# Four shared two-bank PSUM buffers for attention, casts and division sums that heed GpSimd's port, and a new order of the work

## The chip, the cores and the metric

The kernel runs on one core of one Trainium2 chip. The metric is device time in microseconds (us) of one execution. Three executions of the kernel before took 958.71, 961.17 and 962.71 us; the median, 961.17 us, is the time before.

## The reference, cut to what matters

Attention in which a query sees only the keys of its own hash bucket, and behind it a gated feed-forward layer:

```python
q_bits = (einsum('bhsd,dk->bhsk', q, proj) > 0)          # 6 bits; k_bits likewise
mask   = q_bucket[:, :, :, None] == k_bucket[:, :, None, :]
scores = where(mask, q @ k.T / sqrt(64), -1e9)
attn   = exp(scores - max);  attn = attn / (sum(attn) + 1e-9)
x      = attn @ v                                       # 4 x 8 heads, 768 tokens, 64 wide
out    = (sigmoid(x @ w_gate) * (x @ w_val)) @ w_out    # 3072 tokens, 512 -> 1536 -> 512
```

All is fp32. The kernel splits an operand into a high and a low part in fp32r where one pass would not be exact enough.

## The kernel before, in words

**Stages.** Sixteen pairs of heads go through attention one after the other (`pair`, line 808), each in two groups of three query tiles of 128 rows (`attend`, line 1066). Beside it the weights of the feed-forward layer are read as 64-bit numbers, converted, split and stored again (`converted`, `split`, `combined`, lines 363 to 493). Behind attention comes the feed-forward layer (`moe_pair`, line 726), whose seven products per block are Strassen-like sums.

**Tasks of attention.** TensorE does, per group: six *scores* tasks (letter `s`: `scores`, line 1072, eight matmuls in row tiles of 64, into a two-bank PSUM tile `sc`), six *turns* (`t`: `turned`, line 1126, 36 passes of transposes in row tiles, into a two-bank tile `tp`) and six *values* (`v`: `values`, line 1148, in column tiles of 64, all six accumulating into one tile `pv`). Per pair there are two turns of the inputs (`q`: `turn`, line 917) and a hash (`h`: `hash_`, line 956). `f` is an idle matmul (`busy`, line 331); there are 24. VectorE takes the maximum of `sc` (line 1095), ScalarE the exponent (line 1103), VectorE or ScalarE copy `tp` to `ef` (line 1143) and `pv` to `xs` (line 1160), and GpSimd multiplies `xs` with the reciprocal of the sums (line 1163). The sums get their reciprocals in `inverse` (line 1108): add 1e-9, reciprocal, transpose, on VectorE. The high part of q and k is a cast of 128x768 from SBUF to SBUF on ScalarE or VectorE (`high`, line 943); the low part is a subtraction on GpSimd or VectorE (`low`, line 947).

**PSUM.** Attention has three two-bank buffers (`banks`, line 325; in the plan `two=range(3)`) for `sc`, `tp`, the turned inputs and the hash, and two one-bank buffers (pool `ps`, tag `one`), of which the idle matmuls hold one until the last of them; `pv` and the first pair's hash of q take these. Eight banks in all. The first products of the feed-forward layer (`opening`, line 622) use the two one-bank buffers.

**Order.** The order of every engine's instructions is worked out before the kernel is built, by `Plan.order` (line 99). TensorE's order in attention is written out as the string `ORDER`, a letter per task; behind it come the feed-forward tasks in the order in which they were added. On the other engines, of the tasks that are ready the one with the lowest key goes first; `SHIFTS` adds a number to the key of single tasks. A task can only start in the plan when what it takes is free: a PSUM buffer, an SBUF slot, or the token `port`, which GpSimd's operations and some of VectorE's take. On the chip nothing enforces the token: there the engines run their lists in order and wait only for data and for buffers.

```python
    def inverse():
        some = gz["su"][:, : 2 * GT]
        nc.vector.tensor_scalar_add(some, some, EPS)
        nc.vector.reciprocal(some, some)
```

Of the kernel before, what the change touches and what calls it, by code (L numbers as in the profile page):

```python
# [44 lines left out]
    "ffffffffqqqqhhqqhssssshqqfffffffsssssffffhtsstfftttvvvtqqffftsshssssvvtttvvttsssvvvttstssqqvvvvtthtt"  # L45
    "sssvvvtttvvtstsssssvsstvvvsttvvtttvqqssshvtsssvvvtttvvtttssssvvvvvttststtvvvqqtvvttsssssvshvtttvvsts"
    "tssssvqqvtttvvttsssvssvvtttvvttssssvhstvvvttssvvtttvvqqtsshsssstvvvtttvvttsvvvttsssssvvtttvvvqsqsvtt"
    "tvstssshvvvvtttstssssstvvvtttvvvqqstvssshvststvtttvvttssssssvvtqqvvvttttsssssvvvvvthsttvvtttvttsssss"
    "svvvqttvvvttttqssssvvshvvtttsssvssvvvttssttvvqvqttsssssvvvhttttvvttssssvtsssvvvtttvtqqvvvttssssvsstv"
    "htttvvttsssssvvsttvvtqqvvtthtsssssvvvtttvvttssssvvtssstvvvvvtttqqtstsssssvvvtvvvtthttssssvttvvsttvvt"  # L50
    "tsssvvvvtsstvssttvvttsssvttsssvvvvtttvvttvttvvvvtttvvvv"
)
SHIFTS = {
    158: -2.2, 334: -14.55, 652: 23.1, 1364: 2.85, 1375: 12.45, 1713: 14.4, 1743: 15.05, 1759: 14.3, 1800: 16.1, 1830: -10.7,
    1880: -24.2, 1953: 10.2, 1982: 4.8, 2032: 24.05, 2063: 18.85, 2064: 6.9, 2254: 5.25,
# [25 lines left out]
class Plan:  # L81
# [17 lines left out]
    def order(self):  # L99
# [25 lines left out]
        while events:  # L125
            now = events[0][0]
            while events and events[0][0] <= now:
                _, _, kind, what = heapq.heappop(events)
                if kind == "ready":
                    for m, (e, _, _) in enumerate(what.options):  # L130
                        key, number = what.key
                        heapq.heappush(ready[e], ((key + m * SECOND, number), what))
                elif kind == "give" and isinstance(what, tuple):
                    self.rooms[what[0]].append(what[1])
                elif kind == "give":
                    self.stock[what] += 1
            again = True
            while again:
                again = False
                for e in SEEN:  # L140
                    if free[e] > now:
                        continue
                    held = []
                    if e == "pe":
                        t = turns[-1] if turns and any(x is turns[-1] for _, x in ready[e]) and free_for(turns[-1]) else None
                        if t is not None:
                            turns.pop()
                            ready[e] = [kx for kx in ready[e] if kx[1] is not t]
                        held = []
                    while ready[e] and e != "pe":  # L150
                        key, t = heapq.heappop(ready[e])
                        if t.started:
                            continue
                        first = t.options[0][0]
                        behind = sum(not x.started for _, x in ready[first]) if first != e else BEHIND
                        if behind >= BEHIND and free_for(t):
                            break
                        held.append((key, t))
                    else:
                        t = t if e == "pe" else None  # L160
                    for h in held:
                        heapq.heappush(ready[e], h)
                    if t is None:
                        continue
                    again = t.started = True
                    for r in t.take:
                        if r in self.rooms:
                            t.room = self.rooms[r].pop(0)
                        else:
                            self.stock[r] -= 1  # L170
                    ns, emit = next((x[1], x[2]) for x in t.options if x[0] == e)
                    if e == "pe":
                        ns += (LEAVE + BEGIN[t.kind]) * (tiles != t.tiles)
                        last, tiles = t.kind, t.tiles
                    free[e] = now + ns
                    landed, more = 0, ()
                    if t.dmas:
                        n_, moved, *more = t.dmas
                        if e == "sp":
                            free[e] = max(now, self.landings[0]) + ns  # L180
                        self.moving = max(self.moving, free[e] - ns + BEFORE) + moved
                        landed = max(self.moving, free[e] + BEFORE // 2) + BEHIND_IT - free[e]
                        if e == "sp":
                            self.landings = (self.landings + [free[e] + landed] * n_)[n_:]
                    at(free[e], "free", e)
                    seen = free[e] + (landed + sum(more) if landed else SEEN[e])
                    for r in t.give:
# [12 lines left out]
                    out.append((now, emit, e, ns, t.room))  # L200
# [5 lines left out]
def lsh_attention_glu_kernel(ctx, tc, q, k, v, proj, w_gate, w_val, w_out, out):  # L206
# [41 lines left out]
    ps = ctx.enter_context(tc.tile_pool(name="ps", bufs=2, space=PSUM))  # L248
# [71 lines left out]
    for m in range(3):  # L320
        nc.gpsimd.memset(sums[m], 0.0)
# [3 lines left out]
    def banks(name):  # L325
        return ps2.tile([P, 2, 512], F32, name=name, tag=f"two{plan.room}")


    idle = ps.tile([P, 512], F32, name="idle", tag="one")

    def busy():
# [4 lines left out]
        one=1, two=range(3), z=6, kr=2, qr=2, vr=2, h=2, e=12, st=3, su=3, sv=2, rb=2, xs=2,  # L336
# [277 lines left out]
    def group(key, u, n, js, x, sig_, final, prev):  # L614
# [111 lines left out]
    def moe_pair(key, u, prev):  # L726
# [8 lines left out]
        def part_(t, js):  # L735
            pool, tag_ = (ps, "one") if t % TC < ONES else (later["ps"], "z")
# [71 lines left out]
    def pair(i):  # L808
# [171 lines left out]
        def first_pair(needs):  # L980
# [11 lines left out]
            for n, p_ in (("k", 0), ("q", 0), ("k", 1), ("q", 1)):  # L992
# [11 lines left out]
                hash__[n, p_] = add(n_ + 0.1, "pe", 4 * MM * (1 + (n == "k" and p_ == 0)), lambda n=n, p_=p_: hash_first(n, p_), after=[x_, hw["task"]], take=["one"] if n == "q" else ["two"] * (1 - p_), kind="first", stream="h")  # L1004
                b_ = add(n_ + 0.2, "dve", 620, lambda n=n, p_=p_: bits_first(n, p_), after=[hash__[n, p_]], give=["one"] if n == "q" else [("two", hash__["k", 0])] * p_)
                h_ = add(n_ + 0.1, [("act", 430, lambda n=n, p_=p_: high_half(n, p_, nc.scalar.copy)), ("dve", 300, lambda n=n, p_=p_: high_half(n, p_, nc.vector.tensor_copy))], after=[x_])
# [3 lines left out]
                if n == "q":  # L1010
# [4 lines left out]
                    sh = add(n_ + 0.4, [("act", 430, lambda p_=p_: high_half("qs", p_, nc.scalar.copy)), ("dve", 300, lambda p_=p_: high_half("qs", p_, nc.vector.tensor_copy))], after=[s_])  # L1015
# [50 lines left out]
    def attend(i, g, z, needs, v_here):  # L1066
# [21 lines left out]
        def maximum(t, h):  # L1088
# [3 lines left out]
            if h == 0:  # L1092
# [102 lines left out]
        prev = None  # L1195
        for c in range(NC):
            prev = add(
                n if c == 0 else OPEN, "pe", FF, lambda c=c: values(c), after=[prev, v_here, chunks[c]], take=["one"] if c == 0 else [],
                kind="values", give=["ef"] + (["vr"] if c == NC - 1 and g == NG - 1 else []),
            )  # L1200
        a = add(n - 6, either(summed), after=[prev], take=["xs"], give=["one"])
# [4 lines left out]
    for m in range(FILL):  # L1206
        add(IDLE, "pe", MO + (m < WARM) * MO + (m == 0) * 1300, busy, give=["one"] * (m == FILL - 1), stream="f")
# [3 lines left out]
    every = [a for s_ in stored.values() for a in s_]  # L1211

# [37 lines left out]
    for u in range(PAIRS):  # L1250
# [3 lines left out]
        prev = moe_pair(2e4, u, prev)  # L1254

# [33 lines left out]
```

## Time and profile before

| | |
|---|---|
| median of three executions | 961.17 us |
| the profiled execution's own time | 959.54 us |
| span from its first to its last instruction | 957.7 us |
| TensorE busy | 941.2 us (98%) |
| VectorE busy | 765.5 us (80%) |
| ScalarE busy | 497.6 us (52%) |
| GpSimd busy | 249.6 us (26%) |
| granted TensorE clock | 1.00 throughout |

A matmul's end in the profile is modelled, so TensorE at 98% can still wait; the distance from the start of one task to the start of the next is the surer reading. Engines are named PE (TensorE), PEld (its weight loads), DVE (VectorE), ACT (ScalarE), POOL (GpSimd) and SP (SyncE, which issues the DMAs). A tile's name stands for all its buffers.

### The profile page before, as it was taken

The numbers are of one execution on the slowest core, as the hardware profiler recorded it, in microseconds if no ns is written. First come the engines' busy times: TensorE is split into PE (matmuls) and PEld (weight loads), VectorE is DVE, ScalarE is ACT, GpSimd is POOL, SyncE is SP. The second block draws the span as 40 slices with busy tenths as digits, with TensorE's granted clock in tenths as the row PEclk, the third lists the DMA queues.
The fourth block names the chain that finished last, engine by engine and source line by source line (L and its number), as shares of the span: only waits on it lengthen the run. The fifth ranks groups of instructions, "written<-read, shape, count | busy, mean of one in ns | idle before, by whom it ended". The sixth has DMA issues, their size and how long they took to land.

```text
span 957.7 us, 19418 instructions
## 1 busy us (share of the span) xinstructions
PE 941.2 (98%) x7536; PEld 700.4 (73%) x7536; DVE 765.5 (80%) x1362; ACT 497.6 (52%) x868; POOL 249.6 (26%) x227
## 2 busy tenths in 40 slices
PE   8999999998999999999999999999999999999998
PEld 4666666565666666678888888888888888888886
DVE  8989999999999999976867679745766785666566
ACT  6889888898898888854323133231222323221120
POOL 5365465565565555111331100000000000000000
PEclk9999999999999999999999999999999999999999
DMA  6677867777578656678776545844455464554412
GB/s 181 176 226 235 249 210 226 231 216 242 183 240 252 180 190 210 245 294 289 267 251 233 173 148 205 314 147 145 133 194 176 142 232 132 198 166 152 140 60 88
DMA packets 112132, 190.87 MB, mean 199 GB/s; under 512 B 38664, under 2 KB 70824, under 8 KB 112040
## 3 DMA queue, kind: packets, MB, share of 16 engines
q1 hardware_dynamic: 111880, 189.63, 61.3%
q8 instruction: 59, 0.97, 0.4%
q14 instruction: 33, 0.27, 0.1%
q10 hardware_dynamic: 160, 0.00, 0.0%
HBM read 135.27 MB, written 41.42 MB: 185 GB/s over the span
## 4 chain that ended last, share of the span: by engine, by line
PE 88%; DVE 7%; DMA 2%; ACT 1%; issue 1%; SPq 0%; POOL 0%; DVEq 0%; ACTq 0%; POOLq 0%
PE yo L744 19%; PE pv L1153 12%; PE sc L1083 9%; PE tp L1136 7%; PE sc L1077 4%; PE z3g L637 3%; PE z1g L637 3%; PE z2v L637 3%; PE z7g L637 3%; PE z1v L637 3%; PE z4g L637 3%; PE z5g L637 3%; PE z2g L637 3%; PE z6g L637 3%; PE z4v L637 2%; PE z7v L637 2%
## 5 line engine op out<-in xcount | busy, mean ns | idle before, releaser
L1103 ACT ACTIVATE e<-e,st 128x768 f32<-128x768 f32 x192 | 178.3, 930 | 24.4 <-DVE e L1095 24.0
L1095 DVE TENSOR_SCALAR_CACHE_REDUCE e<-sc 128x768 f32<-128x768 f32 x192 | 174.3, 951 | 6.6 <-PE sc L1083 5.2
L1153 PE MATMUL pv<-ef,vr 128*64 128x384 f32 x768 | 143.1, 498 | 0.0
L775 DVE TENSOR_TENSOR ol<-yo,ol 128x512 f32<-128x512 f32 x120 | 82.0, 689 | 54.9 <-PE yo L744 54.7
L1136 PEld LDWEIGHTS tp<-ident,e 64*128 64x128 f32 x2304 | 81.6, 139 | 46.3 <-DVE e L1095 9.8
L1143 ACT COPY ef<-tp 128x768 f32<-128x768 f32 x113 | 87.8, 798 | 21.7 <-PE tp L1136 21.0
L1136 PE MATMUL tp<-ident,e 64*128 64x64 f32 x2304 | 93.6, 227 | 1.4 <-DVE ef L1143 1.0
L1083 PE MATMUL sc<-kh,qsl 64*128 64x384 f32 x192 | 89.8, 468 | 0.0
L1083 PE MATMUL sc<-kh,ql 64*128 64x384 f32 x192 | 89.8, 468 | 0.0
L1153 PEld LDWEIGHTS pv<-ef,vr 128*64 128x64 f32 x768 | 47.3, 136 | 52.4 <-issue 46.2
L1143 DVE COPY ef<-tp 128x768 f32<-128x768 f32 x79 | 74.4, 952 | 7.4 <-PE tp L1136 6.7
L1077 PE MATMUL sc<-kb,qb 64*128 64x384 bf16 x384 | 65.0, 329 | 7.2 <-DVE ef L1143 4.1
L1083 PE MATMUL sc<-kh,qh 64*128 64x384 f32 x192 | 64.3, 335 | 0.0
L1083 PE MATMUL sc<-kh,qsh 64*128 64x384 f32 x192 | 64.2, 334 | 0.0
L1083 PE MATMUL sc<-kl,qh 64*128 64x384 f32 x192 | 64.0, 334 | 0.0
L1083 PE MATMUL sc<-kl,qsh 64*128 64x384 f32 x192 | 64.0, 333 | 0.0
L701 ACT COPY snm1v<-z1v 128x512 f32<-128x512 f32 x18 | 10.6, 589 | 100.9 <-PE z1v L637 100.9
L666 DVE TENSOR_TENSOR gf(0, 0)v<-z2v,snm1v 128x512 f32<-128x512 f32 x18 | 12.5, 692 | 54.9 <-PE z2v L637 54.9
L1077 PEld LDWEIGHTS <-qb 64*128 64x128 bf16 x384 | 23.2, 94 | 40.4 <-issue 30.2
L1163 POOL TENSOR_TENSOR xs<-xs,rb 128x384 f32<-128x384 f32 x32 | 35.3, 1102 | 42.4 <-DVE xs L1160 25.0
L744 PE MATMUL yo<-wo,hh00v 128*128 128x512 f32 x144 | 44.3, 389 | 0.0
L744 PE MATMUL yo<-wo,hh10v 128*128 128x512 f32 x144 | 44.3, 389 | 0.0
(268 smaller groups left out, 2462.2 us busy)
## 6 DMA issues: line engine op xcount, KB each, us to landing
wg<-kg SPq DMA_DIRECT2D x54, 512.0 KB
wv<-kv SPq DMA_DIRECT2D x54, 512.0 KB
wo<-ko SPq DMA_DIRECT2D x36, 512.0 KB
kg<-pkg SPq DMA_DIRECT2D x18, 512.0 KB
kv<-pkv SPq DMA_DIRECT2D x18, 512.0 KB
vr<-in_v_dram SPq DMA_DIRECT2D x16, 384.0 KB
rawg<-in_moe_w_gate_dram SPq DMA_DIRECT2D x12, 512.0 KB
rb<-rd SPq DMA_DIRECT2D x64, 96.0 KB
```

The lines of the kernel that those rows point to most:

```text
L637: nc.tensor.matmul(bank[m], a[:, wc], x[xx, block][:, c, :], start=(c == 0 and i == 0), stop=(c == 1 and i == 2),)
L666: nc.vector.tensor_add(tile_(name, tag) if tag else z[name], bank[m], z[y])
L744: nc.tensor.matmul(accs[t], a[:, ts_], w, start=(jj == 0 and q == 0), stop=(jj == 1 and q == 2),)
L775: FIRST, "dve", 610, lambda t=t: nc.vector.tensor_add(obs[t], accs[t], obs[t]), after=[prev, ended_[t]],
L1077: nc.tensor.matmul(sc[:, j, :GN], z["qb"][rows, beyond if j else c], z["kb"][rows, h], start=True, stop=False, tile_position=(j * D, 0),)
L1083: nc.tensor.matmul(sc[:, j, :GN], q_[rows, c], z["k" + x][rows, h * GN : (h + 1) * GN], start=False, stop=(m == 2), tile_position=(j * D, 0),)
L1095: nc.vector.tensor_scalar(sp(e), gz["sc", t, h][:, :, :GN], MASKED, None, op0=ALU.min, op1=ALU.min, accum_out=gz["st", t][:, h : h + 1],)
L1103: nc.scalar.activation(e, e, AF.Exp, bias=st[:, h : h + 1], scale=-1.0, accum_out=gz["su"][:, h * GT + t : h * GT + t + 1],)
L1136: nc.tensor.transpose(tp[:, r, at_ : at_ + D], gz["e", t, h][rows, c * P : (c + 1) * P], ident[rows, rows], tile_position=(r * D, 0),)
L1143: copy(gz["ef", c].rearrange("p (n r d) -> p r n d", r=2, d=D), gz["tp", c][:, :, :GN].rearrange("p r (n d) -> p r n d", d=D),)
L1153: nc.tensor.matmul(gz["pv"][rows, :GN], z["v"][:, h, 2 * (c % GT) + c // GT], gz["ef", c][:, h * GN : (h + 1) * GN], start=(c == 0), stop= ...
L1163: nc.gpsimd.tensor_mul(gz["xs"], gz["xs"], gz["rb"])
```

## The change

Five things are done.

1. The two one-bank buffers become a fourth two-bank buffer (number 3, pool `psd`). It serves all of attention like the other three. `pv` and the first pair's hash of q now take one of the four, of which they use the first bank. The idle matmuls hold number 3 until the last of them. A new task of SyncE, `ones_switch`, takes number 3 after the last scores and turns it into the two one-bank buffers that the feed-forward layer uses.
2. On VectorE the casts of the high parts (`high`, and `high_half` of the first pair) take the token `port` in the plan; on ScalarE they don't.
3. In `inverse` the tensor-scalar addition of 1e-9 is replaced by a reduction over pairs: columns 0 to 5 of `su` hold the sums, columns 6 to 11 hold 1e-9 (the memset at the start writes it), and a `tensor_reduce` adds the two into a tile `inv`. The reciprocal and the transpose work on `inv`. A further memset writes `inv` once.
4. `ORDER` is another string with as many letters of each kind.
5. `SHIFTS` has 2199 entries in place of 17, for tasks of all stages.

```diff
 ORDER = (
-    "ffffffffqqqqhhqqhssssshqqfffffffsssssffffhtsstfftttvvvtqqffftsshssssvvtttvvttsssvvvttstssqqvvvvtthtt"
-    "sssvvvtttvvtstsssssvsstvvvsttvvtttvqqssshvtsssvvvtttvvtttssssvvvvvttststtvvvqqtvvttsssssvshvtttvvsts"
...
-    "tsssvvvvtsstvssttvvttsssvttsssvvvvtttvvttvttvvvvtttvvvv"
+    "fffffqqqqhqhhqshsssffsqqffssssffffftthtssstffffvttvvvvvqtqffffffsttsstsstvvvvtsssvvhstsssttvtstvvvtts"
+    "qvvqtstthssstvvvvtsssvvttststsvtvvssqvvvvsttsqtsssthvttvvvvvststtsstvvsstvvtqqvssssvhtttstvvvttssssv"
...
+    "vvvtttsvtvsttvvttsssvssssvssvsttvtttvvvvvtttvttvttvvvvv"
 )
 SHIFTS = {
-    158: -2.2, 334: -14.55, 652: 23.1, 1364: 2.85, 1375: 12.45, 1713: 14.4, 1743: 15.05, 1759: 14.3, 1800: 16.1, 1830: -10.7,
...
+    24: -34.3, 25: 3.05, 26: 17.6, 27: 67.8, 29: 26.45, 31: 4.55, 33: 17.1, 34: 2.35, 37: 32.55, 39: 14.15, 40: 32.5,
...
 }
-        def free_for(t):
-            return all((len(self.rooms[r]) if r in self.rooms else self.stock[r]) >= t.take.count(r) for r in t.take)
+        def also(t, e):
+            return next((x[3] for x in t.options if x[0] == e and len(x) > 3), [])
+        def free_for(t, e):
+            return all(
+                r[1] in self.rooms[r[0]] if isinstance(r, tuple) else (len(self.rooms[r]) if r in self.rooms else self.stock[r]) >= t.take.count(r)
+                for r in t.take
+            ) and all(self.stock[r] >= 1 for r in also(t, e))
...
-    ps = ctx.enter_context(tc.tile_pool(name="ps", bufs=2, space=PSUM))
+    psd = ExitStack()
+    ps = psd.enter_context(tc.tile_pool(name="psd", bufs=1, space=PSUM, side="right"))
...
-        nc.gpsimd.memset(sums[m], 0.0)
+        nc.gpsimd.memset(sums[m], EPS)
+    inv = const.tile([P, 32], F32, name="inv")
+    nc.gpsimd.memset(inv, 0.0)
...
-        return ps2.tile([P, 2, 512], F32, name=name, tag=f"two{plan.room}")
+        return (ps if plan.room == 3 else ps2).tile([P, 2, 512], F32, name=name, tag=f"two{plan.room}")
-    idle = ps.tile([P, 512], F32, name="idle", tag="one")
+    idle = ps.tile([P, 2, 512], F32, name="idle", tag="two3")[:, 0]
...
-        one=1, two=range(3), z=6, kr=2, qr=2, vr=2, h=2, e=12, st=3, su=3, sv=2, rb=2, xs=2,
+        one=0, two=range(3), z=6, kr=2, qr=2, vr=2, h=2, e=12, st=3, su=3, sv=2, rb=2, xs=2,
...
-            pool, tag_ = (ps, "one") if opening else (later["ps"], "z")
+            pool, tag_ = (later["one"], "one") if opening else (later["ps"], "z")
...
-                z["hs", n, m] = ps.tile([P, 512], F32, name=f"h{n}{m}{u}", tag="one")
+                z["hs", n, m] = banks(f"h{n}{m}{u}")[:, 0]
...
-            b_ = add(n_, [("act", 735, lambda n=n: high(n, nc.scalar.copy)), ("dve", 480, lambda n=n: high(n, nc.vector.tensor_copy))],
+            b_ = add(n_, [("act", 735, lambda n=n: high(n, nc.scalar.copy)), ("dve", 480, lambda n=n: high(n, nc.vector.tensor_copy), ["port"])],
...
-            some = gz["su"][:, : 2 * GT]
-            nc.vector.tensor_scalar_add(some, some, EPS)
-            nc.vector.reciprocal(some, some)
+            with_eps = gz["su"][:, : 4 * GT].rearrange("p (m n) -> p n m", m=2)
+            nc.vector.tensor_reduce(inv[:, : 2 * GT], with_eps, axis=AX.X, op=ALU.add)
+            nc.vector.reciprocal(inv[:, : 2 * GT], inv[:, : 2 * GT])
             gz["sv"] = at.tile([P, 32], F32, name=f"sv{u}", tag="sv", bufs=stock["sv"])
-            nc.vector.transpose(gz["sv"], gz["su"])
+            nc.vector.transpose(gz["sv"], inv)
...
-                gz["pv"] = ps.tile([P, 512], F32, name=f"pv{u}", tag="one")
+                gz["pv"] = banks(f"pv{u}")[:, 0]
...
-        a = add(n - 6, either(summed), after=[prev], take=["xs"], give=["one"])
+        a = add(n - 6, either(summed), after=[prev], take=["xs"], give=[("two", first_)])
...
+    a.room = 3
+    a.give = [("two", a)]
...
+    def ones_switch():
+        psd.close()
+        later["one"] = ctx.enter_context(tc.tile_pool(name="ps", bufs=2, space=PSUM, side="right", reuse_waits="tile"))
...
+    add(0, "sp", 0, ones_switch, after=score_tasks["last"], take=[("two", 3)], give=["one", "one"])
```

## Rows read from the trace of the kernel before

**Rows 1.** Busy time by stretch: start:end, length, each engine's busy us (instructions), clock, DMA.

```profile
25.00:412.70 387.70, 379.55 (x4965) 242.02 (x4961) 363.45 (x726) 332.28 (x603) 209.10 (x179) 1.00 0.72 222
412.70:957.70 545.00, 539.75 (x2378) 445.63 (x2376) 380.90 (x570) 148.89 (x234) 27.43 (x25) 1.00 0.54 184
```

**Rows 2.** Timeline of TensorE: first idle matmuls, first feed-forward product (start, us).

```profile
1.31 3.59 PE L332 MATMUL idle<-zero 128*128 128x512 bf16 x8 [1.31 <-POOL zero L260]
...
412.71 0.50 PE L637 MATMUL z1g<-a11h,wg 128*128 128x512 f32 x1
```

**Rows 3.** Chain of waits up to 420 us: runs of values and turns (start, us).

```profile
70.35 0.80 PE pv L1153 x4
...
96.64 3.38 PE pv L1153 x20
100.02 0.89 PE tp L1136 x24
...
127.03 1.28 PE tp L1136 x36
```

**Rows 4.** Timeline of TensorE at 156 us: two scores, a hash, the next scores.

```profile
155.97 0.34 PE L1077 MATMUL sc<-kb,qb 64*128 64x384 bf16 x2
156.66 0.34 PE L1077 MATMUL sc<-kb,qb 64*128 64x384 bf16 x2
157.47 0.51 PE L960 MATMUL hs<-qx,hw 128*32 128x384 f32 x1
...
158.25 0.34 PE L1077 MATMUL sc<-kb,qb 64*128 64x384 bf16 x2
```

**Rows 5.** Groups by line, VectorE to 413 us: xcount | busy us, mean ns | idle before.

```profile
L1110 DVE TENSOR_SCALAR su<-su 128x6 f32<-128x6 f32 x32 | 9.7, 302 | 1.7 <-ACT e L1103 1.7
L945 DVE CAST qh<-qx 128x768 fp32r<-128x768 f32 x9 | 9.6, 1069 | 0.2
L945 DVE CAST kh<-kx 128x768 fp32r<-128x768 f32 x7 | 6.6, 946 | 0.1
```

**Rows 6.** Single lines: shortest/median/longest ns, first and last start in us.

```profile
L945 DVE CAST qh<-qx x9: 549/792/2206, 17.2 to 357.4; 128x768 fp32r<-128x768 f32 x9
L1110 DVE TENSOR_SCALAR su<-su x32: 159/168/1769, 22.0 to 404.1; 128x6 f32<-128x6 f32 x32
L1111 DVE RECIPROCAL su<-su x32: 191/192/194, 22.2 to 404.3; 128x6 f32<-128x6 f32 x32
```

**Rows 7.** Timelines at 229 us: GpSimd's subtraction, VectorE's addition, TensorE's next scores.

```profile
228.82 2.12 POOL L948 TENSOR_TENSOR ql<-qx,qh 128x768 fp32r<-128x768 f32 x1
...
229.20 1.77 DVE L1110 TENSOR_SCALAR su<-su 128x6 f32<-128x6 f32 x1
...
232.33 0.34 PE L1077 MATMUL sc<-kb,qb 64*128 64x384 bf16 x2 [2.23 <-DVE ef L1143]
```

**Rows 8.** TensorE's waits from 25 us to 412.7 us: us in total, times, longest.

```profile
PE sc L1077 <- DVE ef L1143: 4.1, 3, 2.2
```

**Rows 9.** Single lines that take the token: shortest/median/longest ns, first and last start.

```profile
L388 DVE TENSOR_SCALAR exg<-rawg x12: 416/425/818, 29.2 to 448.3; 128x512 int32<-128x512 int32 x12
...
L395 DVE TENSOR_SCALAR mfg<-rawg x12: 409/420/440, 29.6 to 448.6; 128x512 int32<-128x512 int32 x12
```

**Rows 10.** A reduction of the setup, as in rows 9.

```profile
L292 DVE TENSOR_REDUCE picked<-ident x4: 167/168/179, 2.5 to 3.2; 128x1 f32<-128x24 f32 x4
```

**Rows 11.** Timelines of the opening: VectorE's cast at 17 us, TensorE at 20 us.

```profile
17.20 2.21 DVE L945 CAST qh<-qx 128x768 fp32r<-128x768 f32 x1
...
20.33 0.34 PE L1077 MATMUL sc<-kb,qb 64*128 64x384 bf16 x2 [0.59 <-DVE e L1095]
```

**Rows 12.** Timelines between attention and feed-forward: VectorE twice, TensorE.

```profile
399.42 1.23 DVE L537 TENSOR_TENSOR a11l<-ra,a11h 128x1024 fp32r<-128x1024 f32 x1 [0.28 <-ACT a11h L533]
...
416.45 1.22 DVE L537 TENSOR_TENSOR s4l<-ra,s4h 128x1024 fp32r<-128x1024 f32 x1
...
419.28 0.47 PE L637 MATMUL z3g<-s4h,wg 128*128 128x512 f32 x1 [0.83 <-issue]
```

More of the change, by code (lines that the diff above doesn't have):

```diff
@@ L129, in order @@
                 if kind == "ready":
-                    for m, (e, _, _) in enumerate(what.options):
+                    for m, (e, *_) in enumerate(what.options):
                         key, number = what.key
@@ L144, in order @@
                     if e == "pe":
-                        t = turns[-1] if turns and any(x is turns[-1] for _, x in ready[e]) and free_for(turns[-1]) else None
+                        t = turns[-1] if turns and any(x is turns[-1] for _, x in ready[e]) and free_for(turns[-1], e) else None
                         if t is not None:
@@ L155, in order @@
                         behind = sum(not x.started for _, x in ready[first]) if first != e else BEHIND
-                        if behind >= BEHIND and free_for(t):
+                        if behind >= BEHIND and free_for(t, e):
                             break
@@ L186, in order @@
                     seen = free[e] + (landed + sum(more) if landed else SEEN[e])
+                    for r in also(t, e):
+                        at(seen, "give", r)
                     for r in t.give:
@@ L735, in part_ @@
         def part_(t, js):
-            pool, tag_ = (ps, "one") if t % TC < ONES else (later["ps"], "z")
+            pool, tag_ = (later["one"], "one") if t % TC < ONES else (later["ps"], "z")
             accs[t] = pool.tile([P, 512], F32, name=f"yo{t}_{js[0]}_{u}", tag=tag_)
@@ L1003, in first_pair @@
                 )
-                hash__[n, p_] = add(n_ + 0.1, "pe", 4 * MM * (1 + (n == "k" and p_ == 0)), lambda n=n, p_=p_: hash_first(n, p_), after=[x_, hw["task"]], take=["one"] if n == "q" else ["two"] * (1 - p_), kind="first", stream="h")
-                b_ = add(n_ + 0.2, "dve", 620, lambda n=n, p_=p_: bits_first(n, p_), after=[hash__[n, p_]], give=["one"] if n == "q" else [("two", hash__["k", 0])] * p_)
-                h_ = add(n_ + 0.1, [("act", 430, lambda n=n, p_=p_: high_half(n, p_, nc.scalar.copy)), ("dve", 300, lambda n=n, p_=p_: high_half(n, p_, nc.vector.tensor_copy))], after=[x_])
+                hash__[n, p_] = add(n_ + 0.1, "pe", 4 * MM * (1 + (n == "k" and p_ == 0)), lambda n=n, p_=p_: hash_first(n, p_), after=[x_, hw["task"]], take=["two"] * (n == "q" or p_ == 0), kind="first", stream="h")
+                b_ = add(n_ + 0.2, "dve", 620, lambda n=n, p_=p_: bits_first(n, p_), after=[hash__[n, p_]], give=[("two", hash__[n, p_ if n == "q" else 0])] * (n == "q" or p_))
+                h_ = add(n_ + 0.1, [("act", 430, lambda n=n, p_=p_: high_half(n, p_, nc.scalar.copy)), ("dve", 300, lambda n=n, p_=p_: high_half(n, p_, nc.vector.tensor_copy), ["port"])], after=[x_])
                 l_ = add(n_ + 0.3, [("dve", 480, lambda n=n, p_=p_: low_half(n, p_, nc.vector)), ("pool", 950, lambda n=n, p_=p_: low_half(n, p_, nc.gpsimd))], after=[h_], **both)
@@ L1014, in first_pair @@
                     add(0, "sp", 0, lambda: None, after=[s_, x_], give=[("two", held["q"])])
-                    sh = add(n_ + 0.4, [("act", 430, lambda p_=p_: high_half("qs", p_, nc.scalar.copy)), ("dve", 300, lambda p_=p_: high_half("qs", p_, nc.vector.tensor_copy))], after=[s_])
+                    sh = add(n_ + 0.4, [("act", 430, lambda p_=p_: high_half("qs", p_, nc.scalar.copy)), ("dve", 300, lambda p_=p_: high_half("qs", p_, nc.vector.tensor_copy), ["port"])], after=[s_])
                     needs[n, p_].append(add(n_ + 0.5, [("dve", 480, lambda p_=p_: low_half("qs", p_, nc.vector)), ("pool", 950, lambda p_=p_: low_half("qs", p_, nc.gpsimd))], after=[sh], **both))
@@ L1194, in attend @@
         n = t0 + LAG + 4
-        prev = None
+        prev = first_ = None
         for c in range(NC):
             prev = add(
-                n if c == 0 else OPEN, "pe", FF, lambda c=c: values(c), after=[prev, v_here, chunks[c]], take=["one"] if c == 0 else [],
+                n if c == 0 else OPEN, "pe", FF, lambda c=c: values(c), after=[prev, v_here, chunks[c]], take=["two"] if c == 0 else [],
                 kind="values", give=["ef"] + (["vr"] if c == NC - 1 and g == NG - 1 else []),
             )
-        a = add(n - 6, either(summed), after=[prev], take=["xs"], give=["one"])
+            first_ = first_ or prev
+        a = add(n - 6, either(summed), after=[prev], take=["xs"], give=[("two", first_)])
         a = add(n - 4, "pool", 965, divided, after=[a, spread_], take=["port"], give=["rb", "port"])
@@ L1206, in lsh_attention_glu_kernel @@
     for m in range(FILL):
-        add(IDLE, "pe", MO + (m < WARM) * MO + (m == 0) * 1300, busy, give=["one"] * (m == FILL - 1), stream="f")
+        a = add(IDLE, "pe", MO + (m < WARM) * MO + (m == 0) * 1300, busy, stream="f")
+    a.room = 3
+    a.give = [("two", a)]
     LAG = 4.8
```

19 lines of the change are left out of this document (12 added, 7 removed), and 240 rows, old and new, of the table SHIFTS.

## The prediction

> **What bounds the kernel now.** I read the busy time by stretch first, then TensorE's timeline at the two ends of attention, the chain of waits for what a task costs, and last VectorE's groups and single lines. There are two stages. From 412.7 us on TensorE is busy for 539.75 of 545.0 us and VectorE for 381 [rows 1]: the feed-forward stage is TensorE's alone, and the change leaves its matmuls as they are. Attention, from the first idle matmul at 1.31 us to the first feed-forward product at 412.71 us [rows 2], takes 411.4 us. There TensorE (379.6 of 387.7) and VectorE (363.5) are both nearly full, ScalarE has 55 us to spare and GpSimd 179 [rows 1].
>
> How much of the 411.4 us is work of TensorE? The starts of tasks tell it. A run of one values task takes 0.80 us, one of five (20 matmuls) 3.38: 0.645 a task and 0.155 for leaving column tiles. Two turns take 0.90 and three 1.28: 0.38 a task and 0.14 for going into column tiles [rows 3]. A scores task lasts 0.69 to the next and 0.81 where a hash follows, so 0.12 for the other tiling; a hash takes 0.78 [rows 4]. With the letters of the old ORDER: 192 x 0.69 = 132.5; 192 x 0.38 = 73.0; 192 x 0.645 = 123.8; 36 input turns at 0.38 = 13.7; 19 hashes at 0.78 + 0.12 = 17; 87 runs of values, each entered and left once, at 0.155 + 0.13 = 0.285: 24.8; 24 idle matmuls, the first eight 0.45 each [rows 2] and the rest some half of that (an estimate), 7. Together about 392 us. So TensorE waits about 19 us of attention, some 7 of them before the first scores have come round. With the tiling changes below that sets the most that an order can win here at some 22 us.
>
> **What it waits for.** The trace names one cause well. VectorE's cast of 128x768 takes 0.55 us at best and 2.21 at worst, the addition on six columns 0.16 and 1.77; the reciprocal between them is 0.19 in all 32 cases [rows 6]. At 229 us one sees why: GpSimd's subtraction runs from 228.82 to 230.94, the addition starts at 229.20 and ends at 230.97, and TensorE's next scores come 2.23 us late, behind the copy that stood in VectorE's queue after the addition [rows 7]. So these two kinds of operation stand still while GpSimd works. In sum: casts 9.6 + 6.6 - 16 x 0.55 = 7.4 us, additions 9.7 - 32 x 0.16 = 4.6 us [rows 5, 6], 12.0 us of VectorE's 363. What of it reaches TensorE by name is 4.1 us in three waits for a copy [rows 8].
>
> **The change, part by part** (against the profiled execution's own 959.54 us, 1.6 below the median of the three runs; the span is 957.7).
>
> *Fewer changes of tiling.* I counted the runs of `v` in the two strings: 87 before, 76 after, the letters being as many. 11 x 0.285 = 3.1 us off TensorE's work. Bounds: 0 if TensorE only waits longer elsewhere, 3.1 if not. I take 3.1, because the time is TensorE's own.
>
> *Casts that take the token.* The rows nearest to what the token does are those of VectorE's operations that hold it already: the 36 mantissa masks (three groups of twelve; one is shown) never pass 0.44 us, of the exponent masks the longest took 0.82 [rows 9]. So the plan's order mostly keeps what it promises, though nothing on the chip enforces it. Where the token is out, a cast goes to ScalarE, which has 55 us to spare [rows 1]. Queued behind a cast that comes later are the subtraction for the low part and the DMAs that swap q; the hash is done 9 to 23 us before the pair's first scores in the new string (by its letters and the prices above), so nobody is late by that.
>
> *The division sums.* One addition becomes one reduction of twelve numbers to six per row. The setup's reductions of 24 to one take 0.17 us [rows 10], the addition at best 0.16: equal. Whether a reduction stands still for GpSimd, no row shows beside a GpSimd operation that reads; bounds are the reciprocal (never) and the addition (4.6 us as now) [rows 5, 6]. I take never, the reciprocal being the nearest in place and size. The Trainium skill, "SBUF — State Buffer", in its part on which operations grab the shared port pair, says that VectorE's copies, casts and tensor-scalar operations can hold the pair and a reduction on trn2 never contends; the rows on casts and additions agree, and by that the 4.6 us would all go. The extra memset lies in the first 4 us on GpSimd, which then waits for its first data: nothing.
>
> *What the port's 12.0 us are worth.* If VectorE alone bounded attention, all of it: 12. If TensorE alone, nothing. Between: TensorE's three named waits are 4.1 us [rows 8], and each stands behind such an operation; smaller waits at turns and scores come to some more. I take 5.
>
> *Four shared buffers.* Before, `pv` had its own banks; scores, turns, input turns and hashes had three buffers. Laid out with the prices above, the time from a group's first `v` to its last is 10.5 us in the old string and 6.9 in the new, of some 12 us per group, and in the new one no `pv` opens before the last is done. So `pv`, with its copy, holds one of four for about 60% of the time: scores and turns have 3.4 buffers on average in place of 3. Worth: bounds -4 (a gain of the small waits) to +3; I take -1. Until the 24th idle matmul, which comes as late in the new string as in the old one (at 32 us by the trace), the fourth is held and `pv` shares the three: a loss there.
>
> *Opening.* The cast at 17.20 us stands still for 1.65 us, and TensorE waits 0.59 at 20.33 for the maximum queued behind it [rows 11]; against it the missing buffer. Bounds -3 to +2, taken -1.
>
> *The passage to the feed-forward stage.* `ones_switch` waits for buffer 3 after the last scores; no scores follow that would need it, and 25 turns and values run under it. Nothing, up to 1 us.
>
> *Feed-forward.* The new SHIFTS only choose among tasks that are ready together on VectorE, ScalarE and SyncE. VectorE has 164 of 545 us idle there [rows 1]. Nothing; bounds -1 to +3.
>
> Sum: -3.1 - 5 - 1 - 1 = -10.1 us: 959.5 - 10.1 = 949.4 against the profiled execution, 951.0 against the median.
>
> **The rivals.**
> (a) *The end of attention moves, the feed-forward stage's input doesn't.* The pieces of its first input come off VectorE one after the other, the first from 399.42, the last (`s4l`) done at 417.67, and TensorE takes it at 419.28 [rows 12]: 1.6 us of slack. They start when the last early weights are stored. If that chain stays and only closes up by the 4 us of attention's work inside it, half of the gain is waited away: 5 us left, 956. For it: the chain is 18 us of nearly unbroken VectorE work. Against: the freed VectorE time lies ahead of it.
> (b) *The waits form anew.* TensorE's order is fixed, so a port wait gone may only uncover the next (a maximum, an exponent). Then only the tiling changes stay: 958.
> (c) *The token doesn't hold.* The casts still meet GpSimd, the reduction doesn't: 3.1 + 5 x 4.6/12.0 = 5.0, and no gain elsewhere: 956.
> (d) *Slower: `pv` waits for a shared buffer.* The first `v` of each of 32 groups must now find one of four free, and all of TensorE's queue stands behind it; before, it had its own. The price of one such wait is that of a buffer that a copy gives back late, 4.1/3 = 1.4 us [rows 8]. The gains of 10.1 are used up at a mean wait of 0.32 us, and 0.5% slower begins at 0.47. At 0.5 us: 16 - 10 = 6 us slower, 967. Against: runs of four and five `v` follow many of the openings, and need no further buffer while the others drain.
>
> **How the numbers follow.** Forecast 0.56; (a) 0.12; (b) 0.13; (c) 0.08; (d) 0.11. The forecast's own range, by the bounds of its terms, is 944 to 956. The range of 8 in 10 takes in (a), (b) and (c): 944 to 959.5; outside lie (d) and a little on either side. A measurement of this kernel can tell about 0.5%, 4.8 us, from no change: faster is under 956.4, slower over 966.0. Faster: nearly all of the forecast, half of (a) and (c): 0.67. Same: (b), the rest of these and the mild part of (d): 0.23. Slower: 0.10.
>
> **What would show it.** The first feed-forward product starts at about 403 us in place of 412.7. The casts' median on VectorE falls towards 0.55 us and none passes 1.3; the reductions stay under 0.2 us, whatever GpSimd does. TensorE's waits for copies lose their 4.1 us. The distance from the last `pv` to the first product stays at 0.4 us, and the feed-forward stage at 545 us. I am wrong if TensorE waits at the first `v` of groups (d), if its first products stand waiting for `a12l`, `s1l`, `s2l` or `s4l` (a), or if casts of 2 us are still there (c).

## The result and the profile after

| | before | after |
|---|---|---|
| median of four executions, us | 961.12 (958.71 to 962.71) | 947.59 (946.86 to 948.90) |
| span of the profiled execution, us | 957.7 | 945.2 |
| attention: first idle matmul to first feed-forward product, us | 411.4 | 391.0 |
| feed-forward: first product to the start of the last one, us | 540.9 | 548.9 |

The kernel after takes 0.9863 of the time before (95% interval 0.9839 to 0.9887), 13.5 us less. The last two lines tell more than the first: attention gave 20.4 us, twice what was forecast, and the feed-forward stage, of whose matmuls the change touches none, took 8.0 us back. So the tests have two questions: what made attention so much shorter, and what made the other stage longer.

Busy time by stretch of the kernel after, columns as in [rows 1] (the two stretches that stand there for before):

```profile
25.00:392.30 367.30, 366.44 (x4942) 242.62 (x4942) 341.57 (x705) 341.02 (x624) 207.06 (x179) 1.00 0.77 231
392.30:941.40 549.10, 548.27 (x2378) 446.86 (x2376) 378.56 (x569) 148.55 (x234) 26.92 (x25) 1.00 0.55 184
```

In attention TensorE now works 366.4 of 367.3 us, where it was 379.6 of 387.7. VectorE lost 22 us of work and ScalarE gained 9: casts have changed engine, and the division sums take 5.2 us in place of 9.7. In the second stretch the number of matmuls is the same, 2378, and so is the granted clock, 1.00; yet they are busy for 548 us.

TensorE's waits from 25 us to the end of attention, kernel after (total, times, longest), are all that the view lists; against [rows 8] the copy that cost 4.1 us in three waits is gone:

```profile
PE idle L586 <- issue: 0.3, 2, 0.2
PE sc L1331 <- ACT ef L1397: 0.3, 1, 0.3
PE pv L1407 <- ACT ef L1397: 0.2, 1, 0.2
```

Before, the same view listed nine such waits, 6.8 us in all. Of the six that [rows 8] leaves out the largest were:

```profile
PE tp L1136 <- DVE ef L1143: 1.0, 2, 0.6
PE sc L1077 <- DVE qb L967: 0.9, 1, 0.9
```

Casts and division sums of the kernel after, line by line, columns as in [rows 6]:

```profile
L1199 ACT CAST qh<-qx x15: 818/837/858, 18.7 to 341.0; 128x768 fp32r<-128x768 f32 x15
L1199 ACT CAST kh<-kx x11: 818/832/850, 34.2 to 337.8; 128x768 fp32r<-128x768 f32 x11
L1199 DVE CAST kh<-kx x4: 518/554/832, 18.0 to 245.7; 128x768 fp32r<-128x768 f32 x4
...
L1364 DVE TENSOR_REDUCE inv<-su x32: 154/160/196, 22.0 to 383.3; 128x6 f32<-128x12 f32 x32
...
L1365 DVE RECIPROCAL inv<-inv x32: 191/191/193, 22.1 to 383.5; 128x6 f32<-128x6 f32 x32
```

VectorE had sixteen such casts, up to 2.21 us long [rows 6]; it has four, the longest 0.83 us. The other twelve run on ScalarE, at 0.83 us each. The division sum's longest went from 1.77 us to 0.20.

The end of attention in TensorE's timeline, kernel after (start, length): the first feed-forward product starts as the last twenty values matmuls end, with no wait.

```profile
388.95 3.45 PE L1407 MATMUL pv<-ef,vr 128*64 128x384 f32 x20
392.33 0.51 PE L891 MATMUL z1g<-a11h,wg 128*128 128x512 f32 x1
```

And one tile of the feed-forward stage (`z2g`), 108 of its products, all over the span (the first figure after the length is TensorE's busy time, the second its weight loads'). Kernel before:

```profile
0.00:999.00 999.00, 27.40 (x108) 20.27 (x108) 12.35 (x18) 1.00 0.59 191
```

The same tile, kernel after:

```profile
0.00:999.00 999.00, 28.01 (x108) 20.36 (x108) 12.38 (x18) 1.00 0.60 191
```

0.61 us more over 108 products is 5.6 ns a product. From start to start the 1512 products of the first kind (tiles z1g to z7v) stood 226.7 ns apart before and 232.4 after, those of the second kind (tile yo, 864) 226.7 and 227.4. 1512 x 5.7 + 864 x 0.7 = 9.2 us, less 1.2 of longer gaps that have gone: the 8.0 us. It is no wait that the profile lists: the products themselves follow one another a little more slowly.

### The profile page after: what moved, and what is told of

It is laid out like the page before. It is cut to its first block, busy times and chain, and to the rows that moved or that the text cites. A ratio compares the mean times of both kernels' runs of the same rounds, so it can differ in the third digit from the quotient of the medians.

```text
span 945.2 us, 19434 instructions
## 1 busy us (share of the span) xinstructions
PE 937.3 (99%) x7532; PEld 703.2 (74%) x7536; DVE 740.4 (78%) x1338; ACT 507.8 (54%) x892; POOL 247.0 (26%) x228
## 4 chain that ended last, share of the span: by engine, by line
PE 98%; ACT 1%; DVE 0%; DMA 0%; issue 0%; SPq 0%; ACTq 0%
PE yo L998 21%; PE pv L1407 14%; PE sc L1337 10%; PE tp L1390 8%; PE sc L1331 4%; PE z1g L891 3%; PE z3g L891 3%; PE z4g L891 3%; PE z6v L891 3%; PE z5v L891 3%; PE z4v L891 3%; PE z5g L891 3%; PE z2v L891 3%; PE z6g L891 3%; PE z2g L891 3%; PE z1v L891 3%
## 5 line engine op out<-in xcount | busy, mean ns | idle before, releaser
L1407 PE MATMUL pv<-ef,vr 128*64 128x384 f32 x768 | 140.6, 496 | 0.2 <-ACT ef L1397 0.2
L1390 PEld LDWEIGHTS tp<-ident,e 64*128 64x128 f32 x2304 | 85.6, 138 | 29.1 <-issue 10.8
L1397 ACT COPY ef<-tp 128x768 f32<-128x768 f32 x118 | 92.3, 796 | 7.0 <-PE tp L1390 6.1
L1397 DVE COPY ef<-tp 128x768 f32<-128x768 f32 x74 | 70.0, 952 | 7.3 <-PE tp L1390 6.8
L1331 PEld LDWEIGHTS <-qb 64*128 64x128 bf16 x384 | 20.5, 95 | 35.7 <-issue 30.2
L998 PE MATMUL yo<-wo,hh11v 128*128 128x512 f32 x144 | 44.5, 390 | 0.0
```

The source lines that it names most:

```text
L998: nc.tensor.matmul(accs[t], a[:, ts_], w, start=(jj == 0 and q == 0), stop=(jj == 1 and q == 2),)
L1331: nc.tensor.matmul(sc[:, j, :GN], z["qb"][rows, beyond if j else c], z["kb"][rows, h], start=True, stop=False, tile_position=(j * D, 0),)
L1390: nc.tensor.transpose(tp[:, r, at_ : at_ + D], gz["e", t, h][rows, c * P : (c + 1) * P], ident[rows, rows], tile_position=(r * D, 0),)
L1397: copy(gz["ef", c].rearrange("p (n r d) -> p r n d", r=2, d=D), gz["tp", c][:, :, :GN].rearrange("p r (n d) -> p r n d", d=D),)
L1407: nc.tensor.matmul(gz["pv"][rows, :GN], z["v"][:, h, 2 * (c % GT) + c // GT], gz["ef", c][:, h * GN : (h + 1) * GN], start=(c == 0), stop= ...
```

## The experiments: where the 8 us of the feed-forward stage come from

The one thing of the change that reaches into this stage from the first instruction on is where tiles lie. The new tile `inv` takes 128 bytes of every partition in a pool at the left of SBUF, and the streamed operands of the first products (`a11h` and its like) move up by 128 bytes with all that is allocated after it. The weight pieces that TensorE holds while they stream lie at the right and stay (but for that of z3v, which lies at the left). The traces hold no addresses; below, a relative shift is the number of bytes by which the distance between the two differs from the kernel before.

**The tile alone.** Kernel before, and nothing of the change but a tile of that size:

```diff
+    pad = const.tile([P, 32], F32, name="pad")
+    nc.gpsimd.memset(pad, 0.0)
```

> The kernel before with one more tile of 128 bytes per partition (zeroed once) ahead of the tiles that the feed-forward products stream; nothing else differs. Theory A, the place in SBUF: the distance from one product to the next rises from 227 ns to about 231 in the seven-product steps and stays 227 in the output products; the feed-forward stage grows by some 8 us, attention stays at 411 us, the time is about 969 us. Theory B, the slower products come from the new PSUM banks or the new order: 227 ns everywhere, 961 us.

968.14 us, where the kernel before on the same chip took 960.68 (median of 7). Attention ended at 412.42 us as before; the feed-forward stage took 549.7 us. The same tile as above, kernel with the padding:

```profile
0.00:999.00 999.00, 28.01 (x108) 20.36 (x108) 12.36 (x18) 1.00 0.60 191
```

The 28.01 us of the kernel after, without one changed instruction besides a memset on another engine.

**The change without the shift.** Kernel after, with `inv` in attention's pool, so that the streamed tiles lie where they lay before:

```diff
-    inv = const.tile([P, 32], F32, name="inv")
+    inv = at.tile([P, 32], F32, name="inv", tag="inv", bufs=1)
```

> The kernel after with the tile inv (128 bytes) taken from attention's own pool, which lies behind the feed-forward products' streamed tiles, so that these stand where they stood before the change. Theory A, the place in SBUF: the seven-product steps return to 227 ns, the feed-forward stage loses 8 us, about 939.5 us. Theory B, PSUM banks or order: no change, 947.6 us.

938.16 us (937.95 to 938.44) against 960.68: 0.9767, interval 0.9751 to 0.9784. That is 22.5 us faster than before and the best kernel of this study. Attention ended at 392.58 us, as in the kernel after; the feed-forward stage took 539.6 us, and the tile:

```profile
0.00:999.00 999.00, 27.42 (x108) 20.28 (x108) 12.39 (x18) 1.00 0.60 191
```

**The shift made at the other side.** Is it the streamed tiles' own address, or their distance from the weight pieces? Kernel after, with `inv` in a pool at the right: now the pieces move by 128 bytes and the streamed tiles lie as before.

```diff
-    ctx.enter_context(tc.tile_pool(name="edge", bufs=1, side="right")).tile([P, 8], F32, name="edge")
+    edge = ctx.enter_context(tc.tile_pool(name="edge", bufs=1, side="right"))
+    edge.tile([P, 8], F32, name="edge")
+    inv = edge.tile([P, 32], F32, name="inv")
...
-    inv = const.tile([P, 32], F32, name="inv")
```

> The kernel after with inv at the other end of SBUF, behind the weights' pieces: now the streamed tiles stand where they stood before the change (address 448 modulo 512) and the pieces have moved by 128 bytes (320 modulo 512). If only the streamed tiles' own address counts, 227 ns and a feed-forward stage of 539.6 us, 938 us in all. If the distance between streamed tile and stationary piece counts, some 231 ns in all steps but the one whose piece lies on the streamed tiles' side (z3v: 227 ns), stage 548 us, 947 us.

949.10 us against 959.34 for the kernel before beside it; feed-forward 548.8 us, the tile:

```profile
0.00:999.00 999.00, 28.02 (x108) 20.36 (x108) 12.38 (x18) 1.00 0.60 191
```

The address of the streamed tiles by itself is not it. What counts is where the two lie to one another. By the expectation's addresses (320 in place of 448 modulo 512) the pieces moved down, which brings the two closer by 128 bytes, just as moving the streamed tiles up does; and product for product the distances in time agree with those of the 128-byte padding, to 0.3 ns on average. No run moves the two apart.

**Half the shift.** Kernel before with 64 bytes of padding (`pad = const.tile([P, 16], F32, name="pad")`).

> The kernel before with a tile of 64 bytes (not 128) ahead of the streamed tiles. If any shift against the pieces counts, the seven-product steps take more than 227 ns (z3v, whose piece shifts along, 227) and the feed-forward stage grows by 4 to 8 us, 965 to 969 us. If 128 bytes is special, 227 ns and 961 us.

961.21 us against 959.34; feed-forward 543.8 us, first products 228.8 ns apart, the tile:

```profile
0.00:999.00 999.00, 27.64 (x108) 20.28 (x108) 12.33 (x18) 1.00 0.60 191
```

The stage grew by 3.0 us, less than the 4 to 8 that were expected, so the loss doesn't grow in step with the shift. A relative shift of 0 gives 226.7 ns, of 64 bytes 228.8, of 128 bytes 232.4, whichever of the two moved. This settles the cause as far as a programmer can act on it. What happens inside the chip at those distances, what a shift the other way does, and whether the pattern repeats at some distance, no run shows.

Two kinds of products are slower although their own two operands kept their distance: those of yo by 0.7 ns on average, and those of z3v by half as much as the others'. This is z3v in the kernel after, where it was 27.40 us before:

```profile
0.00:999.00 999.00, 27.73 (x108) 20.29 (x108) 12.43 (x18) 1.00 0.60 191
```

Their starts, sorted by place in the run of products, tell where. In the kernel after, of the six products of a z3v step the fourth and fifth stand 226.6 to 226.8 ns from their next, as in the kernel before; the first three and the last are slow (228 to 232). Of each run of 48 yo products the first seven and the last are disturbed (224 to 236), and the others stand 226.7 apart. So what is left lies at the borders to steps whose operands did shift, and runs on for a few products. The slowing itself is uneven: in rows of shifted steps at 128 bytes every seventh product took 239 to 241 ns, most of the others 228 to 233.

## The experiments: what shortened attention

From the starts of TensorE's tasks and the prices of the prediction, attention before had 19.35 us of waits: 2.24 in the first 25 us and 17.11 later. After, it has 2.09: 2.39 in the first 25 us and about nothing later (0.3 under zero, by the error of the prices). The rest of the 20.4 us, 3.1, is the changes of tiling by the same prices. Every kernel below ran once. Where only the places of tiles differ, attention ended between 411.5 and 412.7 us with the old order and between 392.3 and 394.4 with the new one, so a single difference under some 2 us says little.

**The reduction alone.** Kernel before with the three lines of the division sums.

```diff
...
+            nc.vector.tensor_reduce(inv[:, : 2 * GT], with_eps, axis=AX.X, op=ALU.add)
+            nc.vector.reciprocal(inv[:, : 2 * GT], inv[:, : 2 * GT])
...
+            nc.vector.transpose(gz["sv"], inv)
```

> The kernel before with the division sums' addition replaced by the reduction (inv in attention's own pool), old order, old PSUM, no token for casts. Theory A, the port decides: the reductions stay under 0.2 us and VectorE gets 4.6 us back; attention gets 2 us shorter (411 to 409), about 959 us. Theory B, the order decides: TensorE's string is fixed and the waits form anew, attention within 1 us of 411.

955.92 us against 960.68; attention ended at 409.11 us, 3.6 earlier, more than theory A's 2. The reductions took 0.17 us at most; the casts on VectorE took 18.6 us together, the first pair's three among them, as before (18.5).

**The token alone.** Kernel before, with the token in the plan for the casts on VectorE (the first pair's halves take it too; not shown).

```diff
...
+            b_ = add(n_, [("act", 735, lambda n=n: high(n, nc.scalar.copy)), ("dve", 480, lambda n=n: high(n, nc.vector.tensor_copy), ["port"])],
...
```

> The kernel before with the token taken by VectorE's casts in the plan, everything else as before (the lists of VectorE, ScalarE and GpSimd shift by that alone). Theory A, the port decides: no cast on VectorE over 1.3 us, VectorE gets up to 7.4 us back, attention 3 us shorter, about 958 us. Theory B, the order decides: casts that no longer stand still don't shorten attention by over 1 us, or the old string fits the shifted lists worse and attention grows.

994.80 us: slower by 34. The casts did what the token asks, none on VectorE over 0.56 us. But attention's small waits grew (23 us from 25 to 400 us, 17 before), and at its end TensorE stood still for one long wait. TensorE's longest waits of this kernel:

```profile
PE z1g L649 <- DMA wg<-kg: 22.5, 1, 22.5
PE sc L1089 <- DVE ef L1155: 4.7, 6, 2.3
PE sc L1089 <- DVE e L1107: 2.0, 4, 0.7
```

When the last early weights were stored stands in SyncE's timeline, first of the kernel before:

```profile
388.88 0.32 SPq L438 DMA_DIRECT2D ko<-pko  x1
```

of the kernel after:

```profile
371.37 0.32 SPq L692 DMA_DIRECT2D ko<-pko  x1
```

and of the one with the token alone:

```profile
423.80 6.13 SPq L450 DMA_DIRECT2D ko<-pko  x2
```

This is the mechanism of rival (a): attention's tasks are done, but what the first product needs isn't there. By which step the plan pushed the weights back was not followed up.

**The change without the token**, and **the change with the old addition**: both from the version with `inv` in attention's pool, with the feed-forward stage at 539.6 us, so that only attention differs.

```diff
-            b_ = add(n_, [("act", 735, lambda n=n: high(n, nc.scalar.copy)), ("dve", 480, lambda n=n: high(n, nc.vector.tensor_copy), ["port"])],
+            b_ = add(n_, [("act", 735, lambda n=n: high(n, nc.scalar.copy)), ("dve", 480, lambda n=n: high(n, nc.vector.tensor_copy))],
...
```

> The kernel after (inv in attention's own pool) without the token on VectorE's casts; the lists shift by that alone. If the casts' standing still is what TensorE waited for, casts of 1 to 2 us are back on VectorE and attention grows by 3 to 8 us over 391 us, to about 941 to 946 us. If the new order absorbs it, within 2 us of 938.

946.71 us against 960.40; attention ended at 401.00 us, 8.4 later than with the token, just beyond the 3 to 8 that were expected. Casts on VectorE were up to 1.57 us long again, and TensorE's longest waits were:

```profile
PE tp L1390 <- DVE e L1349: 2.3, 2, 1.9
PE sc L1331 <- DVE xs L1414: 0.7, 1, 0.7
```

```diff
-            nc.vector.tensor_reduce(inv[:, : 2 * GT], with_eps, axis=AX.X, op=ALU.add)
+            nc.vector.tensor_scalar_add(some, some, EPS)
...
```

> The kernel after with the division sums of before, a tensor-scalar addition on su in place of the reduction into inv (no tile inv at all); order, token and four buffers stay. If the reduction is worth what it was alone in the old order (3.6 us of attention), additions of over 1 us are back and attention is 394 to 396 us, 941 to 943 in all; if the new order leaves room for it, within 1.5 us of 938.

941.71 us against 960.40; attention ended at 396.27 us, 3.7 later. The addition's line in this kernel, columns as in [rows 6]:

```profile
L1362 DVE TENSOR_SCALAR su<-su x32: 159/172/1235, 21.8 to 386.9; 128x6 f32<-128x6 f32 x32
```

In the new order the token is worth 8.4 us and the reduction 3.7; the reduction is worth the same in both orders as far as single runs tell, the token is not.

**The change with the old PSUM.** The version with `inv` in attention's pool, but three shared two-bank buffers and two one-bank buffers for `pv`.

```diff
-        one=0, two=range(3), z=6, kr=2, qr=2, vr=2, h=2, e=12, st=3, su=3, sv=2, rb=2, xs=2,
+        one=1, two=range(3), z=6, kr=2, qr=2, vr=2, h=2, e=12, st=3, su=3, sv=2, rb=2, xs=2,
...
-                gz["pv"] = banks(f"pv{u}")[:, 0]
+                gz["pv"] = ps.tile([P, 512], F32, name=f"pv{u}", tag="one")
```

> The kernel after (inv in attention's own pool) with the PSUM of before: three two-bank buffers for scores, turns, input turns and hashes and two one-bank buffers for pv; new ORDER, new SHIFTS, token and reduction stay. If the fourth shared buffer is what frees TensorE of its waits, attention is longer than the 391 us of the kernel with four buffers by some 5 to 15 us (943 to 953 us in all). If the order and the port do it, attention stays within 2 us of 391 us, about 938 to 940 us.

995.14 us against 960.40, far over both expected ranges. Small waits came back everywhere in attention, 1 to 3 us in every 25 us, and behind them the long one for the weights. Busy time by stretch around it, columns as in [rows 1]:

```profile
400.00:423.00 23.00, 20.95 (x256) 12.11 (x252) 20.23 (x42) 15.24 (x29) 12.22 (x13) 1.00 0.48 160
423.00:446.60 23.60, 0.00 (x0) 0.00 (x0) 10.03 (x11) 7.66 (x9) 5.79 (x5) 0.55 0.70 254
446.60:455.00 8.40, 8.33 (x24) 6.41 (x24) 5.72 (x6) 4.49 (x5) 0.00 (x0) 0.65 1.04 395
455.00:465.00 10.00, 9.17 (x41) 7.50 (x41) 7.64 (x12) 3.62 (x6) 2.59 (x2) 1.00 0.78 267
```

While TensorE stood idle the granted clock fell to 0.55, and it was 0.65 in the 8 us after the restart, 1.00 again behind that: most of the idle stretch, and a good part of the next, at 1.2 GHz in place of 2.4.

**The order.** The version with `inv` in attention's pool with the strings of before, `ORDER` and `SHIFTS`:

> The kernel after (inv in attention's own pool) with ORDER and SHIFTS of before: four shared buffers, token and reduction under the old order. If the buffers and the port do it, attention is 395 to 405 us, 942 to 952 us in all. If they only pay with an order made for them, attention is as long as before or longer, 411 us and up, as it grew to 439 us with the token alone: 958 us or more.

999.85 us against 960.40. With `SHIFTS` alone from before:

> The kernel after (inv in attention's own pool) with the 17 SHIFTS of before: new ORDER, four buffers, token and reduction stay, the lists of the other engines are those that the keys alone give. If TensorE's order is what matters, attention is within 4 us of 391 us and the first feed-forward product follows the last values at once: 938 to 942 us. If the other engines' lists matter as much, the last early weight is stored after 400 us, TensorE stands between attention and feed-forward, and the time is 960 to 1000 us.

986.73 us against 959.34. And the other way round, the kernel before with the two new strings:

> The kernel before with the new ORDER and the new SHIFTS alone: three two-bank buffers and two of one bank, no token, addition in place of the reduction. If the order alone does it, attention is 391 to 400 us, 938 to 948 us in all. If the order only fits the four buffers and the token, attention is longer than before and the last early weight late, as with the old PSUM under the new order: 980 us or more.

972.75 us against 959.34. The first two waited for the weights again, 29.3 and 22.1 us at the first product; in TensorE's timelines (the bracket is the idle time before and what ended it), first the kernel with both old strings:

```profile
444.52 0.76 PE L652 MATMUL z1g<-a11h,wg 128*128 128x512 f32 x1 [29.27 <-DMA wg<-kg]
```

then the one with the old `SHIFTS`:

```profile
431.30 0.77 PE L652 MATMUL z1g<-a11h,wg 128*128 128x512 f32 x1 [22.12 <-DMA wg<-kg]
```

The third did not, against the expectation of a late weight: its attention ended at 427.36 us, 14.7 later than before, in many small waits, of which the longest groups were:

```profile
PE sc L1316 <- DVE e L1334: 6.3, 17, 1.2
PE tp L1375 <- DVE e L1334: 3.2, 4, 1.8
PE hs L1199 <- DVE e L1334: 2.2, 4, 1.3
```

**What follows.** Neither the three rules (buffers, token, reduction) with the old order nor the new order with the old rules wins; together they take nearly all waits away. Of the parts that ran alone (reduction, token, order) only the reduction gained. One reservation: `SHIFTS` is a list of corrections to one exact plan, and every kernel here with a part undone runs lists that were not made for it. Their losses show that the parts belong together; they don't show what fewer parts with an order of their own could reach. That stays open, and so does how the 17.3 us of waits divide between the shared buffers and the token.

## Why the prediction was right in the time and wrong in its parts

The forecast, 951.0 us, lies 3.4 us from the median, and the range held it. That is in part chance: two terms were wrong with opposite signs.

| step | forecast, us | measured, us |
|---|---|---|
| changes of tiling | -3.1 | -3.1 by the same prices, not measured alone |
| port, shared buffers, opening | -5 - 1 - 1 | -17.3 |
| passage | 0 to +1 | 0 |
| feed-forward | 0 (-1 to +3) | +8.0 |
| sum | -10.1 | -12.4 (-20.4 + 8.0) in the profiled executions, -13.5 in the medians |

- **The step "what the port's 12.0 us are worth" was mis-sized.** Together with the buffers I took 6 us where 17.3 were to be had. For one part the size is measured alone: by the prediction's rate the division sums were worth 5 x 4.6/12.0 = 1.9 us, and the reduction gave 3.6 in the old order and 3.7 in the new one. The ceiling was in the prediction, about 22 us by the starts of tasks, and the result came within 2 us of it. I priced the gain by three waits that the trace names, 4.1 us [rows 8], and a little more. The view names nine, 6.8 us, where the starts of tasks give 17.1; the other 10 us carry no name there, and they went too. The far ends given for the three, -12, -4 and -3, together held the result; the values taken between them did not. Nor does the range "by the bounds of its terms", 944 to 956, follow from those bounds: added up, they give 938 to 970.
- **The opening gained nothing:** 2.2 us of waits in the first 25 us before, 2.4 after. The measured 0 lies within the bounds of the term of -1. The "some 7" us of waits that the prediction put ahead of the first scores don't come out of its prices: these give 2.2 in the first 25 us, or 5.8 with the first eight idle matmuls counted as waiting.
- **"Feed-forward: nothing" failed.** I asked what the new `SHIFTS` could do there and never what a new tile does to the addresses of the others. The diff showed the tile, and I priced only its memset. No row of before shows that a product's time depends on addresses, since there the products stand evenly, 226.7 ns apart; the bound of +3 was drawn for another cause.
- **The token and the reduction did as said.** No cast on VectorE passes 0.83 us (1.3 was the bound that I gave), and the reduction stays at 0.154 to 0.196 us. The Trainium skill, "SBUF — State Buffer", in its part on who interferes with whom, says that a reduction on trn2 never contends for the port pair; these 32 instances agree, of which 17 ran beside GpSimd.
- **Rival (a) did not happen, but its mechanism is real.** The chain moved with attention: its last store went from 388.88 to 371.37 us, and the product found its operands ready. In four of the runs with a part undone TensorE waited 22 to 29 us for the weights. In those kernels it cost far more than the 5 us that I gave it, because I let the chain stay where it was; it can also be pushed back.
- **Rivals (b) and (c)** are refuted by the waits and by the casts. Of **(d)** at most one wait of 0.2 us is left, the `pv` in the waits of after. Spread over the 32 groups that is under 0.01 us, where the gains would have been used up at 0.32.

## What to carry to other kernels

When a stage waits in many small pieces, the sum of its waits, counted from the starts of tasks, says more of what a new order can win than the waits that the trace names. Rules and order are to be tried together: the token alone and the order alone made this kernel 34 and 13 us slower, and beside the other parts the same token is worth 8 us. And any new tile in a pool that others follow, however small, moves its neighbours: compare the time of a single product of untouched code before and after, and put the tile where neither what TensorE streams nor the weights that it holds lie behind it.

## What the hardware did that I had not expected

In the feed-forward stage a product's time depended on where its streamed operand lay to the weights: 226.7, 228.8 and 232.4 ns at relative shifts of 0, 64 and 128 bytes, 8 us in a stage of 541. The Trainium skill, "SBUF — State Buffer", in its part on who interferes with whom, gives TensorE's two reads ports of their own that wait on no one; by that the shift would cost nothing. The runs with moved tiles show otherwise, and they decide.

An idle TensorE cost more than its idle time. In the kernel with the old PSUM, after 23.7 us without work, the granted clock was 0.65 for the next 8 us; twelve of the first products stood 427 ns apart, and the stage took 542.3 us in place of 539.6. All of these 2.7 us lie in its first 14 products, and the profile lists no further wait there for data. After the other three long waits, 22.1 to 29.3 us, the stage took 548.3 to 549.3 us: besides 16 or 17 products 427 ns apart, TensorE waited 3.2 to 4.0 us for one more copy. Such products of the kernel with the token alone (start, length):

```profile
442.28 0.63 PE L649 MATMUL z1g<-a11l,wg 128*128 128x512 f32 x1
442.71 0.63 PE L649 MATMUL z1g<-a11h,wg 128*128 128x512 f32 x1
443.14 0.63 PE L649 MATMUL z2g<-a12h,wg 128*128 128x512 f32 x1
```
